# RWKV attention and top-1 experts on one core: when r and k are loaded, how row buffers are cleared and held, and the order of some VectorE steps

## The chip, the cores and the metric

The kernel runs on one core of a Trainium2 chip. A core has TensorE (matmuls, from SBUF into the banks of PSUM), VectorE, ScalarE and GpSimd (called PE, DVE, ACT and POOL in the profile), SyncE (SP), which here only issues transfers, and 16 DMA engines that move data between the chip's HBM and SBUF. The metric is the device time of one execution in microseconds (us), the median of several runs.

## What is computed

The reference is a linear attention with decay, followed by a layer of experts where each token goes to one expert. All data is float32.

```python
B, H, S, D = 4, 8, 768, 48           # batch, heads, sequence, head size
for t in range(S):                   # attention
    cur = einsum('bhd,bhe->bhde', u[None] * kt, vt)
    y[:, :, t] = einsum('bhd,bhde->bhe', rt, state + cur)
    state = w[None, :, :, None] * state + einsum('bhd,bhe->bhde', kt, vt)

x = y.transpose(0, 2, 1, 3).reshape(3072, 384)
logits = x @ w_gate                  # 8 experts
expert_idx = argmax(logits, axis=1)
gate_w = softmax(logits)[arange(3072), expert_idx]
for e in range(8):
    xe = x[expert_idx == e]
    out[expert_idx == e] = gate_w[...] * (maximum(xe @ w1[e], 0) @ w2[e])   # 384 -> 1024 -> 384
```

## The kernel before

The order of the work on every engine is the order in which the program is written: nothing is rescheduled. An engine runs its instructions one after the other, and each waits on semaphores for what it needs.

**Attention.** A turn `i` of the loop from L732 handles one unit: one batch `b` and one pair of heads `hp`, 16 units in all (U), four for each batch. Six chunks of 128 tokens are worked at once. In turn i:

- SP loads r and k of unit i + 3 (`load_rk`, L91) into one of three tiles `rks`, at the turn's beginning, and v and k of unit i + 3 (`load_vk`, L96) into one of four tiles `vks`, at its end. r and k come as 112 rows of 6 KB: 48 of the first head, 16 rows of zeros, 48 of the second. The arrays are laid out like that by the host. The three first loads are issued before the loop, load 3 at L720.
- TensorE makes the terms of a token with itself (`p_own`), the scores of each chunk (`p_scores`, L297), turns the outputs of unit i - 2 (`p_tr`, L358), makes the states (`p_ds`, L320), and the outputs of unit i - 1 (`p_out`, L340 and L345).
- VectorE scales r and k of unit i + 1 by the decays (`scale`, L266), lays the scores into masked matrices (`mask`), and scans the states. GpSimd forms r times k of unit i + 1 (`pairs`, L272) and scales its keys (`keys`, L276).
- ScalarE writes the diagonals (`diag`, L303), copies the outputs of unit i - 2 into a tile of rows (`keep`, L362), and copies the outputs of unit i - 1 from PSUM.

The tile of rows `xbs[b % 2]` collects the finished tokens of one batch from its four units. When a batch is full, VectorE picks each token's expert (`choose`, L368) and its place among that expert's tokens (`slots`), and GpSimd scatters the rows, 128 tokens at a time, to an array `rows` in HBM that has an area for each expert (`send`, L410; `sends` gives the turns: those of batch b in turns 4b + 6 to 4b + 9). The part of each area between rows 320 and 416 is cleared first (`clear`, L115, in turn 4), since a pass reads a fixed number of rows for each expert.

**Experts.** Two short passes `early` of 160 tokens for experts 0 and 1 fill the end of the attention. Eight passes `late` follow, k = 0 to 7, one for each expert and of a fixed width: `WIDTH` is 224, 192, 416, 412, 408, 396, 380, 364 (the loop from L905). While pass k does its first layer, the kernel has the second layer of pass k - 1 (called `o`) still to do.

From pass 2 on the first layer goes in four quarters (`quarter`, L493): a 2 x 2 product of blocks with seven instead of eight products, which takes sums of weight blocks `quart[q]` (`quarter_sums`, L533: five VectorE operations for a quarter) and sums of token blocks `toks` (`token_sums`, L545: four operations). The sums of pass k + 1 are made by VectorE during pass k: those of quarter q - 2 after quarter q, the rest after the last quarter, behind the transposes `xT` of pass k + 1's tokens (L470) and its token sums. Within a quarter VectorE does the steps L515, L519, L522, L523 and L525 on what TensorE has left in PSUM, and then the sums of pass k - 1's hidden values (`inner_sums`).

The second layer of the first 256 tokens of pass k - 1 is `tokens_out` (L586), again with seven products. It starts with four small VectorE operations, here called the places (L589 to L594): they compute to which row of the output each token goes, for the two scatters at its end. Then come the products (L603) in five banks ba, bb, bd, be, bf. Bank bf is the same as ba, so the last product waits until VectorE has read ba's second half, in the step `add` at L621. In `tokens_out` of pass 1, which runs after pass 2's quarters, ba and bf are the bank `dsb`.

Of the kernel before, what the change touches and what calls it, by code (L numbers as in the profile page):

```python
# [40 lines left out]
def bc(ap, shape):  # L41
    return ap.to_broadcast(shape)


def straight(tc, rk, vk, w, w1, w2, out, flag):
# [45 lines left out]
    def load_rk(i):  # L91
        if i < U:
            b, hp = divmod(i, HP)
            nc.sync.dma_start(rks[i % 3][0:KP], rk[b, hp].rearrange("h p u s -> (h p) u s")[0:KP])

    def load_vk(i):  # L96
        if i < U:
# [14 lines left out]
    nz = (CAP - PAD) * HP * Q // 128  # L112
    zt = ca.tile([128, nz], FP32, name="zt")

    def clear():  # L115

        nc.gpsimd.memset(zt, 0.0)
        nc.sync.dma_start(rows.rearrange("(e n) c -> e (n c)", e=E)[:, PAD * HP * Q:CAP * HP * Q].rearrange(
            "e (p z) -> p e z", p=128), bc(zt[:, None, :], [128, E, nz]))

    p_fill(17, X01[1][:, 0, :])
    strict = cp.tile([128, C], FP32, name="strict")
# [126 lines left out]
    Ss = [ca.tile([128, D, G - 1], FP32, name=f"S{i}") for i in range(2)]  # L249
    own = [ca.tile([128, G, 32], FP32, name=f"own{i}") for i in range(2)]  # L250
    yTs = [ca.tile([128, 2, S // 2], FP32, name=f"yT{i}") for i in range(3)]
    xbs = [ca.tile([128, G, HP, Q], FP32, name=f"xb{i}") for i in range(2)]
    lg, sub, ex, eq = [ca.tile([128, G, E], FP32, name=n) for n in ("lg", "sub", "ex", "eq")]
    rko = ca.tile([128, G, E], FP32, name="rko")
    mx, se, m2 = [ca.tile([128, G], FP32, name=n) for n in ("mx", "se", "m2")]
# [104 lines left out]

    def keep(i):
        b, hp = divmod(i, HP)  # L362
        nc.scalar.copy(xbs[b % 2][:, 0:4, hp, :], trv[0])
        nc.scalar.copy(xbs[b % 2][:, 4:G, hp, :], trv[1])

    full = [128, G, E]

    def choose(b):  # L368
        oh = ohs[b % 2]
        nc.vector.tensor_reduce(lg, xbs[b % 2][:, :, :, 2 * D:].rearrange("p c a e -> p c e a"), axis=AX, op=ALU.add)  # L370
        nc.vector.tensor_reduce(mx, lg, axis=AX, op=ALU.max)
        nc.vector.tensor_tensor(sub, lg, bc(mx[:, :, None], full), op=ALU.subtract)
        nc.scalar.activation(ex, sub, func=ACT.Exp)

        nc.vector.scalar_tensor_tensor(out=eq, in0=sub, scalar=0.0, in1=bc(rev[:, None, :], full),
                                       op0=ALU.is_equal, op1=ALU.mult)
        nc.vector.tensor_reduce(m2, eq, axis=AX, op=ALU.max)
        nc.vector.tensor_tensor(oh, eq, bc(m2[:, :, None], full), op=ALU.is_equal)
# [10 lines left out]
                             skip_group_check=True)  # L389

    def slots(b):
        oh, xb = ohs[b % 2], xbs[b % 2]
        nc.vector.tensor_tensor(rko, rp, oh, op=ALU.mult)
        with nc.allow_low_precision("whole numbers below 2^24"):
            nc.vector.tensor_reduce(slot[b % 2], rko, axis=AX, op=ALU.add)

    def gates(b):
        xb = xbs[b % 2]
# [11 lines left out]
    def send(b, cs):  # L410
        for c in cs:
            s_ = nc.gpsimd.indirect_dma_start(  # L412
                out=rows[:, :], out_offset=bass.IndirectOffsetOnAxis(ap=slot[b % 2][:, c:c + 1], axis=0),
                in_=xbs[b % 2][:, c].rearrange("p a q -> p (a q)"), in_offset=None, bounds_check=E * N - 1, oob_is_err=False)
            tc.declare_no_dep(s_.ins, group="rows", reason="each token has a row of its own")
            tc.add_to_no_dep_group("rows", s_.ins)

    def ids(b):
        nc.gpsimd.iota(xbs[b % 2][:, :, :, 2 * D + 1].bitcast(I32), pattern=[[4 * C, G], [1, HP]], base=4 * S * b,
                       channel_multiplier=4)  # L420

    def p_count():
# [18 lines left out]
    class Pass:  # L441
# [144 lines left out]
        def tokens_out(self):  # L586

            nt, it2 = self.nt, self.it2
            nc.vector.tensor_scalar(out=vt[:, 0:nt], in0=pos2[:, 0:nt], scalar1=float(self.s0),  # L589
                                    scalar2=bp[:, self.k:self.k + 1], op0=ALU.add, op1=ALU.is_lt)  # L590
            nc.vector.memset(it2[:, 0:nt], 1 << 20)
            nc.vector.tensor_scalar(out=ia[:, 0:nt], in0=self.xg[:, 0:nt, 1].bitcast(I32), scalar1=2, scalar2=None,  # L592
                                    op0=ALU.logical_shift_right)
            nc.vector.copy_predicated(it2[:, 0:nt], vt[:, 0:nt], ia[:, 0:nt])  # L594

            h, ws, g = self.h, w2s[self.k % 2], self.xg[:, :, 0:1]
            Z = DM // 2

            def product(p, at, a, b):
                for f in range(FT // 2):
                    nc.tensor.matmul(p[:, at * Z:(at + 1) * Z], lhsT=a(f), rhs=b(f), start=f == 0, stop=f == FT // 2 - 1,  # L603
                                     skip_group_check=True)
# [12 lines left out]

            y = self.yt

            def add(o, p, at, q):  # L620
                nc.vector.tensor_tensor(o, p[:, at * Z:(at + 1) * Z], q, op=ALU.add)  # L621
# [12 lines left out]
            ba, bb, bd, be, bf = self.banks  # L634
            product(ba, 0, A(0, 0), B_(0, 0))
            product(ba, 1, A(0, 1), B_(1, 0))
            nc.scalar.copy(so[0], ba[:, 0:Z])  # L637
            add(so[1], ba, 1, so[0])
            weigh(place(0, 0), so[1], 0)
            product(bb, 0, Sm(1), Tm(1))  # L640
            product(bb, 1, Sm(0), Tm(0))
            add(so[2], bb, 0, so[0])
            add(so[3], bb, 1, so[2])
            weigh(so[4], so[3], 0)
            weigh(so[5], so[3], 1)
            product(bd, 0, Sm(3), B_(1, 1))
            final(0, 1, bd, 0, so[4])
            scatter(out, it2[:, 0:1], self.yt[0][:, :], N)
            product(be, 0, Sm(2), Tm(2))
            add(so[6], be, 0, so[2])  # L650
            weigh(so[7], so[6], 1)
            final(1, 1, be, 0, so[5])
            product(bf, 0, A(1, 1), Tm(3))
            final(1, 0, bf, 0, so[7])
            scatter(out, it2[:, 1:2], self.yt[1][:, :], N)
# [148 lines left out]
    nc.gpsimd.tensor_copy(turn, xbs[1][0:1, G - 1, 2, 0:1])  # L804
    send(B - 2, range(3, G))
    p_out(U - 1)
    out_t(U - 1)
# [86 lines left out]

    for k, p in enumerate(late):
        o = late[k - 1]
        ahead = k + 1 < n and k > 0
        if k == n - 1:
            o.inner_sums()
# [10 lines left out]
        else:  # L910

            if k < 2:
                if k:
                    o.inner_sums()
                for f in range(FT):
                    p.L1((f,))
                    if f % 2:
                        result(p, f)
            else:
                for q in range(4):  # L920
                    p.quarter(q)
                    o.inner_sums((q,))
                    if q > 1:
                        late[k + 1].quarter_sums(q - 2)
                    if k == 2 and q % 2:
                        result(p, 2 * q - 1)
                p.relus()
            late[k + 1].xT()
            if ahead:
                late[k + 1].token_sums()  # L930
                for q in range(0 if k == 1 else 2, 4 if k < n - 2 else 3):
                    late[k + 1].quarter_sums(q)
            if k == 0:
                okay()
# [528 lines left out]
```

## Time and profile before

The median of six runs is 369.05 us. One more execution was profiled; the profile's numbers are of that one.

| what | value |
|---|---|
| median of 6 runs | 369.05 us (366.51 to 370.15) |
| the profiled execution's own time | 367.62 us |
| its span, first to last instruction | 365.7 us |
| mean granted TensorE clock | 0.995 |
| busy: TensorE, VectorE, ScalarE, GpSimd | 353.0, 261.5, 142.7, 203.8 us |
| HBM read, written | 53.29 MB, 11.40 MB |

The stages in the span: first loads and decays until about 16 us, the attention loop until about 110 us, its end with the early passes until about 142 us, passes 0 and 1 until 160 us, passes 2 to 7 until about 343 us, and the last second layer and scatter until the end.

In the views of the profile L12 is line 12 of the program. `a<-b` means that an instruction writes tile a and reads tile b. A waits view lists, for each engine and line, which engine's step ended the wait, the total in us, how often, and the longest. A line of the timeline gives start, length, engine, line, operation, tiles, shape and count, and in brackets how long the engine idled before it and what ended that. A line of a table of stretches gives the length, then busy time (and number of instructions) of PE, PEld (TensorE's loading of weights), DVE, ACT and POOL, then TensorE's granted clock, the DMA engines' share of busy time and GB/s.

### The profile page before, as it was taken

How to read it: one execution, taken by the hardware profiler on the slowest of the kernel's cores; microseconds unless marked ns; L12 is line 12 of the kernel's file. 1: busy time of each engine (PE TensorE's matmuls, PEld its weight loads, DVE VectorE, ACT ScalarE, POOL GpSimd, SP SyncE). 2: the span in 40 equal slices, each digit the busy share in tenths (PEclk: the TensorE clock that was granted, in tenths of full speed). 3: DMA queues.
4: the chain of work that ended last, by engine and by line, in shares of the span. 5: the costliest groups of instructions: out<-in, count | busy, mean ns of one | idle time of the engine just before them, and what ended most of it. 6: DMA issues, size and time to landing. Idle time of an engine off the chain costs nothing.

```text
span 365.7 us, 9077 instructions
## 1 busy us (share of the span) xinstructions
PE 353.0 (97%) x3355; PEld 334.8 (92%) x3355; DVE 261.5 (72%) x653; ACT 142.7 (39%) x411; POOL 203.8 (56%) x242
## 2 busy tenths in 40 slices
PE   7899999999999999999998999999999999999991
PEld 7688888888889999999998999999999999999891
DVE  6987798798872348674797995896688588685531
ACT  2587878787784301322313312322221231113210
POOL 5387889989865420652116407905922951999341
PEclk9999999999999999999999999999999999999997
DMA  7999997887656976888449327524742953313401
GB/s 202 265 243 233 271 273 244 258 249 231 218 147 205 319 295 124 209 250 229 133 159 213 92 73 213 162 89 152 189 146 91 203 152 125 108 51 100 133 20 50
DMA packets 35205, 65.08 MB, mean 178 GB/s; under 512 B 18617, under 2 KB 19657, under 8 KB 35152
## 3 DMA queue, kind: packets, MB, share of 16 engines
q1 hardware_dynamic: 29648, 49.86, 50.8%
q0 software_dynamic: 3776, 9.84, 7.6%
q10 hardware_dynamic: 1728, 4.72, 3.7%
q8 instruction: 28, 0.46, 0.5%
q14 instruction: 25, 0.20, 0.2%
HBM read 53.29 MB, written 11.40 MB: 177 GB/s over the span
## 4 chain that ended last, share of the span: by engine, by line
PE 90%; DMA 4%; DVE 2%; SPq 1%; POOL 1%; issue 0%; POOLq 0%; DVEq 0%
PE X L501 12%; PE X L563 10%; PE X L479 8%; PE tr L603 7%; PE yps L603 7%; PE X L297 6%; PE yps L340 6%; PE yps L501 5%; PE tr L358 5%; DMA vk<-in_vk_dram 4%; PE yps L345 3%; PE tr L501 3%; PE dsb L501 3%; PE dsb L603 3%; PE yps L563 2%; PE dsb L320 2%
## 5 line engine op out<-in xcount | busy, mean ns | idle before, releaser
L675 POOL DMA_INDIRECT out_dram<-yo,ix x28 | 28.4, 1015 | 67.9 <-DVE ia L592 63.7
L303 ACT ACTIVATE A<-ident,own 128x128 f32<-128x128 f32 x192 | 57.9, 390 | 7.4 <-DVE own L289 7.0
L412 POOL DMA_INDIRECT rows<-xb,slot x24 | 30.3, 1262 | 12.6 <-issue 4.8
L563 PE MATMUL X<-hT,w2s 128*128 128x160 f32 (+5 forms) x288 | 36.5, 287 | 0.0
L563 PEld LDWEIGHTS X<-hT,w2s 128*128 128x128 f32 x288 | 36.2, 191 | 0.2
L603 PE MATMUL yps<-tums,sums 128*128 128x192 f32 x184 | 32.4, 326 | 0.0
L603 PEld LDWEIGHTS yps<-tums,sums 128*128 128x128 f32 x184 | 30.3, 190 | 0.0
L675 POOL DMA_INDIRECT out_dram<-yt,it x16 | 16.8, 1048 | 22.1 <-DVE so L621 10.9
L266 DVE TENSOR_TENSOR RK<-rk,TT 112x1536 f32<-112x1536 f32 x16 | 27.7, 1729 | 2.0 <-DMA rk<-in_rk_dram 2.0
L297 PEld LDWEIGHTS X<-RK 48*128 48x128 f32 x384 | 23.1, 187 | 6.3 <-issue 4.3
L297 PE MATMUL X<-RK 48*128 48x128 f32 x384 | 27.1, 283 | 1.2 <-DVE RK L266 1.2
L272 POOL TENSOR_TENSOR rp<-rk 112x768 f32<-112x768 f32 x15 | 27.3, 1819 | 0.0
L309 DVE COPY_PREDICATED A<-strict,X 128x512 f32<-128x512 int32 x32 | 23.3, 742 | 4.3 <-ACT A L303 4.2
L501 PE MATMUL X<-xT,w1s 128*128 128x208 f32 (+5 forms) x120 | 26.0, 331 | 0.0
L689 POOL TENSOR_TENSOR tums<-w2s,tums 128x384 f32<-128x384 f32 x24 | 24.7, 1029 | 0.4
L340 PE MATMUL yps<-A,vk 128*48 128x128 f32 x384 | 24.0, 274 | 0.0
L501 PEld LDWEIGHTS X<-xT,w1s 128*128 128x128 f32 x120 | 20.9, 190 | 0.0
L340 PEld LDWEIGHTS yps<-A,vk 128*48 128x48 f32 x384 | 20.2, 123 | 0.5
L637 ACT COPY so<-tr 128x192 f32<-128x192 f32 x7 | 2.2, 318 | 44.4 <-PE tr L603 44.4
L689 DVE TENSOR_TENSOR sums<-hT 128x512 f32<-128x512 f32 x16 | 17.1, 1068 | 3.2 <-ACT hT L481 3.2
L603 PE MATMUL tr<-w2s,hT 128*128 128x192 f32 x112 | 19.4, 326 | 0.0
L530 ACT ACTIVATE hT<-hT 128x416 f32<-128x416 f32 (+5 forms) x23 | 12.4, 537 | 17.9 <-DVE hT L522 17.8
(214 smaller groups left out, 828.2 us busy)
## 6 DMA issues: line engine op xcount, KB each, us to landing
w1s<-in_w_dram SPq DMA_DIRECT2D x36, 384.0 KB, 3.3
rk<-in_rk_dram SPq DMA_DIRECT2D x16, 672.0 KB, 8.9
w2s<-in_w_dram SPq DMA_DIRECT2D x24, 384.0 KB, 3.6
vk<-in_vk_dram SPq DMA_DIRECT2D x16, 528.0 KB, 5.5
w2s<-in_w_dram ACTq DMA_DIRECT2D x8, 384.0 KB, 5.7
xs<-rows SPq DMA_DIRECT2D x16, 169.0 KB, 5.3
w1s<-in_w_dram ACTq DMA_DIRECT2D x4, 384.0 KB, 3.6
rows<-zt SPq DMA_DIRECT2D x1, 1248.0 KB, 7.7
```

Of the source, the lines that this page charges most:

```text
L266: nc.vector.tensor_tensor(RKs[i % 3][0:KP].rearrange("p u (c t) -> p u c t", t=C), x[0:KP].rearrange("p u (c t) -> p u c t", t=C), bc(TT[: ...
L272: (eng or nc.gpsimd).tensor_tensor(rps[i % 2][0:KP], x[0:KP, 0], x[0:KP, 1], op=ALU.mult)
L297: nc.tensor.matmul(o, lhsT=r[q, 1, c * C:(c + 1) * C], rhs=r[q, 0, c * C:(c + 1) * C], start=True, stop=True, skip_group_check=True)
L303: nc.scalar.activation(A[:, place(c, h), :], ident, func=ACT.Copy, scale=own[i % 2][:, c, h:h + 1])
L340: nc.tensor.matmul(o(c, h), lhsT=v[:, c, h * D:(h + 1) * D], rhs=A[:, place(c, h), :], start=c < 2, stop=c == 0, skip_group_check=True)
L412: s_ = nc.gpsimd.indirect_dma_start(out=rows[:, :], out_offset=bass.IndirectOffsetOnAxis(ap=slot[b % 2][:, c:c + 1], axis=0), in_=xbs[b % ...
L479: nc.tensor.matmul(p[:, 0:self.n], lhsT=w1s[self.k % 2][f // 2][:, m, f % 2 * 128:(f % 2 + 1) * 128], rhs=self.t[:, m, 0:self.n], start=m ...
L501: nc.tensor.matmul(p[:, at * n:(at + 1) * n], lhsT=a, rhs=b, start=j == 0, stop=j == len(ab) - 1, skip_group_check=True)
L563: nc.tensor.matmul(p[:, 0:n], lhsT=w2s[self.k % 2][f // 2][:, f % 2, m * 128:(m + 1) * 128], rhs=self.h[:, f, self.c:self.n], start=f == 0 ...
L603: nc.tensor.matmul(p[:, at * Z:(at + 1) * Z], lhsT=a(f), rhs=b(f), start=f == 0, stop=f == FT // 2 - 1, skip_group_check=True)
L675: s_ = nc.gpsimd.indirect_dma_start(out=to[:, :], out_offset=bass.IndirectOffsetOnAxis(ap=at, axis=0), in_=x, in_offset=None, bounds_check ...
L689: (eng or nc.vector).tensor_tensor(o, a, b, op=how)
```

## The change

Loads of r and k: the first three are as before. The others bring only the 96 rows that are not zeros, as two transfers of 48 rows, one to partitions 0 to 47 and one to 64 to 111; the 16 rows between keep the zeros of the first three loads. In the loop load 4 is issued at the beginning of turn 1, and load i + 4 in turn i, after GpSimd's product for unit i + 1.

Clearing: instead of one transfer for eight experts in turn 4 there are four for two experts each, at the ends of turns 2 to 5. Tile of rows: three in place of two, so that batch b has `xbs[b % 3]`.

Order of VectorE's steps: in pass 2 (`k == 2`) the sums of pass 3's quarter q - 1 are made after quarter q, in place of those of q - 2, so that one quarter's sums, not two, are left for after the last quarter. In `tokens_out` the places are computed after the three `add` steps on ba and bb instead of at the start, in every pass.

```diff
     def load_rk(i):
         if i < U:
             b, hp = divmod(i, HP)
-            nc.sync.dma_start(rks[i % 3][0:KP], rk[b, hp].rearrange("h p u s -> (h p) u s")[0:KP])
+            if i < 3:
+                nc.sync.dma_start(rks[i % 3][0:KP], rk[b, hp].rearrange("h p u s -> (h p) u s")[0:KP])
+            else:
+                for h in range(2):
+                    nc.sync.dma_start(rks[i % 3][64 * h:64 * h + D], rk[b, hp, h, 0:D])
...
-    def clear():
-        nc.gpsimd.memset(zt, 0.0)
-        nc.sync.dma_start(rows.rearrange("(e n) c -> e (n c)", e=E)[:, PAD * HP * Q:CAP * HP * Q].rearrange(
-            "e (p z) -> p e z", p=128), bc(zt[:, None, :], [128, E, nz]))
+    def clear(e):
+        if not e:
+            nc.gpsimd.memset(zt, 0.0)
+        nc.sync.dma_start(rows.rearrange("(e n) c -> e (n c)", e=E)[e:e + 2, PAD * HP * Q:CAP * HP * Q].rearrange(
+            "e (p z) -> p e z", p=128), bc(zt[:, None, :], [128, 2, nz]))
...
-    xbs = [ca.tile([128, G, HP, Q], FP32, name=f"xb{i}") for i in range(2)]
+    xbs = [ca.tile([128, G, HP, Q], FP32, name=f"xb{i}") for i in range(3)]
...
         def tokens_out(self):
             nt, it2 = self.nt, self.it2
-            nc.vector.tensor_scalar(out=vt[:, 0:nt], ...)
-            nc.vector.memset(it2[:, 0:nt], 1 << 20)
-            nc.vector.tensor_scalar(out=ia[:, 0:nt], ...)
-            nc.vector.copy_predicated(it2[:, 0:nt], vt[:, 0:nt], ia[:, 0:nt])
+            def places():
+                nc.vector.tensor_scalar(out=vt[:, 0:nt], ...)
+                nc.vector.memset(it2[:, 0:nt], 1 << 20)
+                nc.vector.tensor_scalar(out=ia[:, 0:nt], ...)
+                nc.vector.copy_predicated(it2[:, 0:nt], vt[:, 0:nt], ia[:, 0:nt])
...
             add(so[3], bb, 1, so[2])
             weigh(so[4], so[3], 0)
             weigh(so[5], so[3], 1)
+            places()
             product(bd, 0, Sm(3), B_(1, 1))
...
     for i in range(1, U):
         b, k = divmod(i - 6, 4)
         rt = i >= 6 and k == 0 and b < B - 1
-        load_rk(i + 3)
+        if i == 1:
+            load_rk(4)
         p_own(i)
...
             pairs(i + 1)
+            load_rk(i + 4)
             keys(i + 1, nc.vector if i in (7, 8, 11, 12) else None)
...
         load_vk(i + 3)
-        if i == 4:
-            clear()
+        if 2 <= i < 6:
+            clear(2 * i - 4)
...
     for k, p in enumerate(late):
         o = late[k - 1]
+        lag = 1 if k == 2 else 2
...
                 for q in range(4):
                     p.quarter(q)
                     o.inner_sums((q,))
-                    if q > 1:
-                        late[k + 1].quarter_sums(q - 2)
+                    if q >= lag:
+                        late[k + 1].quarter_sums(q - lag)
...
                 late[k + 1].token_sums()
-                for q in range(0 if k == 1 else 2, 4 if k < n - 2 else 3):
+                for q in range(0 if k == 1 else 4 - lag, 4 if k < n - 2 else 3):
                     late[k + 1].quarter_sums(q)
```

More of the change, by code (lines that the diff above doesn't have):

```diff
@@ L362, in keep @@
         b, hp = divmod(i, HP)
-        nc.scalar.copy(xbs[b % 2][:, 0:4, hp, :], trv[0])
-        nc.scalar.copy(xbs[b % 2][:, 4:G, hp, :], trv[1])
+        nc.scalar.copy(xbs[b % 3][:, 0:4, hp, :], trv[0])
+        nc.scalar.copy(xbs[b % 3][:, 4:G, hp, :], trv[1])
     full = [128, G, E]
@@ L369, in choose @@
         oh = ohs[b % 2]
-        nc.vector.tensor_reduce(lg, xbs[b % 2][:, :, :, 2 * D:].rearrange("p c a e -> p c e a"), axis=AX, op=ALU.add)
+        nc.vector.tensor_reduce(lg, xbs[b % 3][:, :, :, 2 * D:].rearrange("p c a e -> p c e a"), axis=AX, op=ALU.add)
         nc.vector.tensor_reduce(mx, lg, axis=AX, op=ALU.max)
@@ L391, in slots @@
     def slots(b):
-        oh, xb = ohs[b % 2], xbs[b % 2]
+        oh, xb = ohs[b % 2], xbs[b % 3]
         nc.vector.tensor_tensor(rko, rp, oh, op=ALU.mult)
@@ L397, in gates @@
     def gates(b):
-        xb = xbs[b % 2]
+        xb = xbs[b % 3]
         nc.vector.tensor_reduce(se, ex, axis=AX, op=ALU.add)
@@ L413, in send @@
                 out=rows[:, :], out_offset=bass.IndirectOffsetOnAxis(ap=slot[b % 2][:, c:c + 1], axis=0),
-                in_=xbs[b % 2][:, c].rearrange("p a q -> p (a q)"), in_offset=None, bounds_check=E * N - 1, oob_is_err=False)
+                in_=xbs[b % 3][:, c].rearrange("p a q -> p (a q)"), in_offset=None, bounds_check=E * N - 1, oob_is_err=False)
             tc.declare_no_dep(s_.ins, group="rows", reason="each token has a row of its own")
@@ L418, in ids @@
     def ids(b):
-        nc.gpsimd.iota(xbs[b % 2][:, :, :, 2 * D + 1].bitcast(I32), pattern=[[4 * C, G], [1, HP]], base=4 * S * b,
+        nc.gpsimd.iota(xbs[b % 3][:, :, :, 2 * D + 1].bitcast(I32), pattern=[[4 * C, G], [1, HP]], base=4 * S * b,
                        channel_multiplier=4)
@@ L588, in tokens_out @@
             nt, it2 = self.nt, self.it2
-            nc.vector.tensor_scalar(out=vt[:, 0:nt], in0=pos2[:, 0:nt], scalar1=float(self.s0),
-                                    scalar2=bp[:, self.k:self.k + 1], op0=ALU.add, op1=ALU.is_lt)
-            nc.vector.memset(it2[:, 0:nt], 1 << 20)
-            nc.vector.tensor_scalar(out=ia[:, 0:nt], in0=self.xg[:, 0:nt, 1].bitcast(I32), scalar1=2, scalar2=None,
-                                    op0=ALU.logical_shift_right)
-            nc.vector.copy_predicated(it2[:, 0:nt], vt[:, 0:nt], ia[:, 0:nt])
+            def places():
+                nc.vector.tensor_scalar(out=vt[:, 0:nt], in0=pos2[:, 0:nt], scalar1=float(self.s0),
+                                        scalar2=bp[:, self.k:self.k + 1], op0=ALU.add, op1=ALU.is_lt)
+                nc.vector.memset(it2[:, 0:nt], 1 << 20)
+                nc.vector.tensor_scalar(out=ia[:, 0:nt], in0=self.xg[:, 0:nt, 1].bitcast(I32), scalar1=2, scalar2=None,
+                                        op0=ALU.logical_shift_right)
+                nc.vector.copy_predicated(it2[:, 0:nt], vt[:, 0:nt], ia[:, 0:nt])
             h, ws, g = self.h, w2s[self.k % 2], self.xg[:, :, 0:1]
@@ L803, in straight @@
     keep(U - 2)
-    nc.gpsimd.tensor_copy(turn, xbs[1][0:1, G - 1, 2, 0:1])
+    nc.gpsimd.tensor_copy(turn, xbs[(B - 1) % 3][0:1, G - 1, 2, 0:1])
     send(B - 2, range(3, G))
```

## The prediction

> **What bounds the kernel now.** I read the page's slices first, then the waits of TensorE, then the chain of waits and VectorE's timeline around the one late wait, then the DMA share of the first stage.
>
> ```profile
> PE   7899999999999999999998999999999999999991
> PEclk9999999999999999999999999999999999999997
> DMA  7999997887656976888449327524742953313401
> ```
>
> A slice is 9.14 us. TensorE is busy at 9 tenths or more from the third slice to the last but one, at full clock; DMA is near full in slices 2 to 8, the attention loop.
>
> ```profile
> PE X L110 <- POOL ident masks.py:199: 1.4, 1, 1.4
> PE X L297 <- DVE RK L266: 1.2, 1, 1.2
> PE dsb L603 <- DVE so L621: 1.2, 1, 1.2
> PE dsb L285 <- POOL rp L272: 0.8, 1, 0.8
> PE dsb L285 <- DVE rp L272: 0.2, 1, 0.2
> ```
>
> All that TensorE waits for, in us. Four of the five lie before 16.2 us, in work that the change leaves alone. The third is at 193 us. So a transfer or another engine is worth time only where it makes TensorE wait, and after 16.2 us that happens once.
>
> ```profile
> 187.33 1.51 DVE xT L470 x3
> 188.84 0.27 DVE toks L689
> 189.13 0.94 DVE toks L689 x3
> 190.30 1.11 DVE quart L689 x5
> 191.44 0.90 DVE quart L689 x4
> 192.33 0.14 DVE vt L589
> 192.75 0.28 DVE so L621
> 193.16 1.54 PE dsb L603 x8
> ```
>
> The chain there (start, length, work; small steps not copied) is all VectorE: after pass 2's last quarter it transposes pass 3's tokens, forms their sums, two quarters' weight sums (10 `quart` operations, 189.98 to 192.25), the places (L589 to L594, 192.25 to 192.66), and only then reads bank `dsb` in L621, which frees it for TensorE's last product.
>
> ```profile
> 177.98 0.59 DVE L515 TENSOR_TENSOR midu<-X,mida 128x416 f32<-128x416 f32 x1 [0.23 <-PE X L501]
> 179.67 0.38 DVE L519 TENSOR_TENSOR midv<-X,midu 128x208 f32<-128x208 f32 x1 [1.10 <-PE X L501]
> ```
>
> In pass 2's third quarter VectorE idles 0.23 and 1.10 us (brackets), waiting for TensorE.
>
> ```profile
> 20.00:30.00 10.00, 9.88 (x168) 8.30 (x166) 8.58 (x12) 8.39 (x27) 8.40 (x7) 1.00 1.04 236
> 39.00:48.00 9.00, 9.00 (x164) 7.45 (x162) 7.00 (x14) 6.41 (x20) 6.84 (x16) 1.00 0.95 297
> rk<-in_rk_dram SPq DMA_DIRECT2D x16, 672.0 KB, 8.9
> vk<-in_vk_dram SPq DMA_DIRECT2D x16, 528.0 KB, 5.5
> rows<-zt SPq DMA_DIRECT2D x1, 1248.0 KB, 7.7
> ```
>
> The last two numbers of a stretch are the DMA share and GB/s. Full-width transfers get about 297/0.95 = 313 GB/s. A turn of the loop is 6.22 us on TensorE (turns 4, 5 and 6 start with L297 at 34.37, 40.59 and 46.81 in the chain).
>
> **The change, part by part.**
>
> *One quarter's sums sooner, places later (pass 2 and after).* Removed from between the last quarter and L621: five `quart` operations, 189.98 to 191.13 in the timeline, 1.13 us, and the four operations of the places, 0.41 us. L621 then starts at 192.66 - 1.13 - 0.41 = 191.12 and ends 0.35 later, at 191.47. TensorE followed it by 0.15 (193.01 to 193.16), so it may go at 191.62. It is ready after the eight matmuls of `tr` begun at 190.54, at 0.162 us each (1.30 per eight in the chain): 191.84. The stall goes entirely, with 0.22 us to spare: **-1.32 us** (193.16 - 191.84). Bounds: 0, if the wait only moves, to 1.32; I take 1.32, of which the sums alone give 1.13 and the places the last 0.19. The five operations now run in the second quarter, before L515 at 177.98. They delay it by 1.13 - 0.23 - 0.08 (the overlap of two operations' spans), so it ends at about 179.4, before TensorE has what L519 needs at 179.67: covered by VectorE's 1.33 us of idle time; each us beyond would push L515 of the fourth quarter, whose bank TensorE takes 0.39 us after it is read (183.65, 184.04). The places now stand before L628, which idles for 0.62 us waiting for ScalarE or TensorE in every pass: nothing.
> What is late next? After 193 TensorE is gapless to 358, so the saving should reach the end.
>
> *r, k in mid-turn and in halves.* 13 loads of 672 KB become 26 of 288 KB: 96 KB less each, 0.31 us of DMA at 313 GB/s. 13 more issues at 0.31 to 0.42 us on SP, which is no link of the chain after 4.2 us. The wait on SP moves: load i+4 is asked for in turn i once POOL's product L272 for i+1 is done, against after the turn's end before; in turn 2 that is 25.6 against 27.0. Queued behind this wait on SP are load i+3 of v, k and the clearing; where POOL scatters rows (L272 ends at 59.18, v, k left at 58.75) they leave about 1 us later. A v, k load asked for at 26.9 is first used by POOL at 38.3: 11.4 us, against landings of 7 to 8.5 in these turns. So there is cover of about 3 us for v, k, and more for r, k. Loads that TensorE never waited for give nothing in this execution. In the loop one thing more: turn 3 took 6.59 us, 0.37 over its neighbours, with weight loading idle for 0.30 at 30.3 that the profile gives to "issue", while the DMA share was 1.0. Whether DMA makes it no row shows: 0 to 0.37, half taken, **-0.19**.
>
> The Trainium skill speaks against the halves: "SBUF — State Buffer", section "Can I just issue two DMAs to hit both halves?", says that transfers to partitions 0 to 63 and 64 to 127 serialize, and its table that half the partitions reach 8 of 16 ports, at 196 GB/s against 328. By that a load would take 2 x 1.5 us against 2.1, an estimate from that page; the sum would stay as it is, since a turn has room for 0.9 us. No run here shows a load of long rows on half the partitions.
>
> *Clearing in four parts.* The same 1248 KB, after turns 2 to 5, three more issues of 0.66 us on SP. POOL's first scatter (54.59) waits for the last part, asked for at about 46 with 1.45 MB at most ahead and in it, 4.6 us at 313 GB/s: about 52. POOL has 0.28 us after that scatter (L272 ends 59.18, TensorE takes it at 59.46). Nothing, with 2 us of cover. POOL's fill of `zt` (0.35 us) is two turns sooner, beside the same idle time.
>
> *Three tiles.* ScalarE's copies L363 and L364 of batch 2 waited on the scatters of batch 0, those of batch 3 on batch 1's. In turn 10 L364 idles 1.09 us against 0.83 in turn 6, perhaps for that; TensorE went from L297 to L340 in 3.84 us in both turn 7 and turn 11. Nothing; covered by ScalarE's idle time.
>
> *Beyond the profiled execution.* It took 367.62 us (span 365.7 and 1.9 around it), 1.43 under the median 369.05. What the other runs have more is not shown. Landings come within 0.1 us of use at 17.1 and 22.0 (third and fourth r, k load), so waits on loads are a candidate: 0 to 1.43, half taken, **-0.72**.
>
> Sum for the profiled execution: 367.62 - 1.32 - 0.19 = 366.1. For the median: 369.05 - 1.32 - 0.19 - 0.72 = **366.8 us**.
>
> **The rivals.**
>
> *B, only the stall at 193 goes*: 369.05 - 1.32 = 367.7. For it: no wait on a load in the profile after 12.4 us. Against: DMA share 1.0 and two landings with no slack.
>
> *C, the sums don't free it*: the five operations push the fourth quarter's L515 past its 0.39 us, or POOL holds VectorE up (one L689 of 0.68 us took 2.98 at 199.5, beside POOL's work). The stall moves: 368.6 to 369.4. Against: POOL does nothing between 176.2 and 182.2.
>
> *D, slower: halves make DMA the bound of the loop.* Small partial loads are slow here: `xs`, 32 partitions, 169 KB in 5.3 us (32 KB/us) against `w1s`, 128 partitions, 384 KB in 3.3 (116 KB/us). Part of that is short runs, so I price half the full rate, 157 GB/s: r, k 590 kB 3.8 us, v, k 541 kB 1.7, and a clearing part or a turn's scatters (320 kB) 1.0: 6.5 against 6.22, and with what 62 to 68 us show (share 0.87 at 257 GB/s, so 295 at most) 6.9. Some 0.68 us in each of 11 turns, 7.5, less 3.4 of cover for v, k: +4.1, so 369.05 - 1.32 + 4.1 = 371.8. It decides once a v, k load takes over 11.4 us to land. Against: 26 smaller transfers keep all engines fed and carry 14% less.
>
> *E, all the unknown waits go*: 369.05 - 1.32 - 0.37 - 1.43 = 365.9.
>
> **How the numbers follow.** Forecast A, 366.8 (its own range 366.0 to 367.5): 0.48; B 0.16; C 0.08; D 0.20; E 0.08. What a measurement of this kernel tells from no change is about 0.5%, 1.85 us: below 367.2 is faster. Of A 0.40 lies there, with E 0.48 faster; the rest of A with B and C is 0.32 within; D is 0.20 slower. The range takes in E, less a little for the spread of runs, and the near end of D: 365.2 to 370.4.
>
> **What would show it.** TensorE's wait "dsb L603 <- DVE so L621" is gone, L621 comes before the places, and from the last quarter of pass 2 to pass 3 is 1.3 us shorter. Turn 3 takes 6.2 to 6.6. VectorE's idle time at L519 in pass 2's third quarter falls from 1.10 to about 0.3. Loads of r, k land in under 10 us. Wrong would be: waits "RK <- DMA rk" or "Kd <- DMA vk" in the loop, turns over 6.3 us, a wait of POOL's first scatter on the clearing, or L603 waiting for another VectorE step.

## The result and the profile after

| | before | changed |
|---|---|---|
| median | 367.41 us (365.9 to 370.32, 79 runs) | 365.47 us (364.8 to 368.94, 37 runs) |
| profiled execution, its span | 367.62, 365.7 us | 365.2, 363.3 us |
| mean granted TensorE clock of that execution | 0.995 | 0.996 |
| HBM read | 53.29 MB | 52.02 MB |

The ratio is 0.9946, 95% interval [0.9932, 0.9961]: by the ratio 1.98 us faster, between 1.4 and 2.5. The six runs shown at first had a median 1.64 us above that of all 79. A run at a mean clock of 0.985 to 0.987 takes some 3 us more than one at 0.992 to 0.997 (367.7 to 368.9 us against 364.8 to 366.7 for the changed kernel), so a median of six can shift with how many of them are such.

What TensorE waits for in the changed kernel (the waits view: total, times, longest, in us):

```profile
PE X L115 <- POOL ident masks.py:199: 1.4, 1, 1.4
PE X L303 <- DVE RK L272: 1.4, 1, 1.4
PE dsb L291 <- POOL rp L278: 0.4, 1, 0.4
PE dsb L291 <- DVE rp L278: 0.2, 1, 0.2
```

The wait of 1.2 us on `so` is gone; the others lie before 16 us. (Lines shift: L297 is now L303, L501 L507, L603 L611, L621 L629, L519 L525.) The chain of waits from the last quarter of pass 2 to pass 3, all TensorE:

```profile
185.54 3.90 PE yps L611 x24
189.44 1.30 PE tr L611 x8
190.74 1.30 PE dsb L611 x8
192.04 3.83 PE X L507 x22
```

The eight matmuls of `dsb`, which had waited until 193.16, follow those of `tr` at once. VectorE's timeline in the same pass:

```profile
178.41 0.37 DVE L525 TENSOR_TENSOR midv<-X,midu 128x208 f32<-128x208 f32 x1 [0.29 <-PE X L507]
...
189.85 0.35 DVE L629 TENSOR_TENSOR so<-dsb,so 128x192 f32<-128x192 f32 x1
190.12 0.74 DVE L629 TENSOR_TENSOR so<-yps,so 128x192 f32<-128x192 f32 x2
...
191.10 0.16 DVE L602 COPY_PREDICATED it<-vt,ia 128x2 int32<-128x2 int32 x1
```

The third quarter's idle time fell from 1.10 to 0.29 us, which is where the five sums went. L629 has read `dsb` at 190.20, 0.54 us before TensorE takes the bank, and the places come after it.

Where the 2.4 us of the span went, by the starts of stages in the two profiles: turn 2 began 0.88 us sooner (20.61 against 21.49), turn 3 took 6.22 instead of 6.59, the first step of pass 2 to that of pass 3 took 24.57 (167.47 to 192.04) instead of 25.97 (168.73 to 194.70), and 0.26 us was lost after 327 us. All other stages agree within about 0.1 us.

The loads in the changed kernel (issues: count, KB, median us to landing):

```profile
vk<-in_vk_dram SPq DMA_DIRECT2D x16, 528.0 KB, 7.7
rk<-in_rk_dram SPq DMA_DIRECT2D x26, 288.0 KB, 6.1
...
rows<-zt SPq DMA_DIRECT2D x4, 312.0 KB, 8.9
```

Halves of r and k land sooner than the whole did (8.9), v and k later (7.7 against 5.5). In this profile TensorE, VectorE's scaling and GpSimd's keys wait for none of them in the loop.

### The profile page after: what moved, and what is told of

It is laid out like the page before. It is cut to its first block, busy times and chain, and to the rows that moved or that the text cites. A ratio compares the mean times of both kernels' runs of the same rounds, so it can differ in the third digit from the quotient of the medians.

```text
span 363.3 us, 9106 instructions
## 1 busy us (share of the span) xinstructions
PE 351.7 (97%) x3355; PEld 333.9 (92%) x3355; DVE 263.7 (73%) x653; ACT 142.8 (39%) x411; POOL 203.9 (56%) x242
## 3 DMA queue, kind: packets, MB, share of 16 engines
HBM read 52.02 MB, written 11.40 MB: 175 GB/s over the span
## 4 chain that ended last, share of the span: by engine, by line
PE 93%; DVE 2%; DMA 2%; POOL 1%; issue 0%; POOLq 0%; SPq 0%; ACT 0%; DVEq 0%
PE X L507 12%; PE X L569 10%; PE yps L611 9%; PE X L485 8%; PE tr L611 8%; PE X L303 6%; PE yps L346 6%; PE yps L507 5%; PE tr L364 5%; PE dsb L611 4%; PE yps L351 3%; PE tr L507 3%; PE dsb L507 3%; PE yps L569 2%; PE dsb L326 2%; PE X L364 2%
## 5 line engine op out<-in xcount | busy, mean ns | idle before, releaser
L611 PE MATMUL yps<-tums,sums 128*128 128x192 f32 x184 | 32.4, 326 | 0.0
L611 PEld LDWEIGHTS yps<-tums,sums 128*128 128x128 f32 x184 | 30.3, 190 | 0.0
L303 PEld LDWEIGHTS X<-RK 48*128 48x128 f32 x384 | 23.1, 187 | 6.6 <-issue 4.3
L303 PE MATMUL X<-RK 48*128 48x128 f32 x384 | 27.1, 283 | 1.4 <-DVE RK L272 1.4
L507 PE MATMUL X<-xT,w1s 128*128 128x208 f32 (+5 forms) x120 | 26.0, 331 | 0.0
L507 PEld LDWEIGHTS X<-xT,w1s 128*128 128x128 f32 x120 | 20.9, 190 | 0.0
L640 ACT ACTIVATE so<-so,xg 128x192 f32<-128x192 f32 x24 | 10.0, 450 | 25.2 <-DVE so L629 25.2
L611 PE MATMUL tr<-w2s,hT 128*128 128x192 f32 x112 | 19.4, 326 | 0.0
```

Of the source, the lines that this page charges most:

```text
L303: nc.tensor.matmul(o, lhsT=r[q, 1, c * C:(c + 1) * C], rhs=r[q, 0, c * C:(c + 1) * C], start=True, stop=True, skip_group_check=True)
L507: nc.tensor.matmul(p[:, at * n:(at + 1) * n], lhsT=a, rhs=b, start=j == 0, stop=j == len(ab) - 1, skip_group_check=True)
```

## The experiments

The kernels ran in four groups (the first four of the table, the next four, the next three, the last), each on one chip together with the kernel before. The chips differ: before took 366.97 us on one and 370.78 to 372.78 on three others. So totals are compared on one chip, and stages within profiles.

| kernel | median us | before, same chip | ratio, 95% interval | pass 2 to pass 3, us |
|---|---|---|---|---|
| sums_and_places | 369.47 | 370.83 | 0.9971 [0.9951, 0.9991] | 24.57 |
| sums_only | 370.06 | 370.83 | 0.9982 [0.9960, 1.0004] | 24.85 |
| places_only | 370.09 | 370.83 | 0.9969 [0.9947, 0.9991] | 25.57 |
| sums_later | 371.15 | 370.83 | 1.0004 [0.9983, 1.0025] | 26.41 |
| after_again | 365.07 | 366.97 | 0.9953 [0.9924, 0.9983] | 24.58 |
| loop_part | 366.93 | 366.97 | 0.9994 [0.9970, 1.0018] | 25.97 |
| first_loads_split | 369.77 | 366.97 | 1.0063 [1.0040, 1.0085] | 24.57 |
| halves_twice | 389.23 | 366.97 | 1.0607 [1.0558, 1.0656] | 24.57 |
| after_whole_rows | 369.05 | 370.78 | 0.9939 [0.9908, 0.9970] | 24.58 |
| whole_twice | 392.96 | 370.78 | 1.0564 [1.0519, 1.0610] | 24.57 |
| start_sooner | 376.02 | 370.78 | 1.0133 [1.0104, 1.0163] | 24.57 |
| decays_sooner | 370.28 | 372.78 | 0.9936 [0.9910, 0.9961] | 24.57 |

### VectorE's order, in four pieces

`sums_and_places` is the kernel before with both changes of VectorE's order and nothing else; `sums_only` and `places_only` have one each; `sums_later` goes the other way, with three quarters' sums left for the end.

```diff
+        lag = 1 if k == 2 else 2          # sums_later: 3 if k == 2 else 2
...
-                    if q > 1:
-                        late[k + 1].quarter_sums(q - 2)
+                    if q >= lag:
+                        late[k + 1].quarter_sums(q - lag)
...
             weigh(so[5], so[3], 1)
+            places()
```

> The kernel before with only the VectorE part of the change (pass 3's sums one quarter sooner in pass 2, the places behind the add steps). Theory (the stall at 193 us is what the change is worth): TensorE's wait 'dsb L603 <- DVE so' is gone, the step from pass 2's last quarter to pass 3 is 1.3 us shorter, and the time is 1.3 us under the kernel before, ratio about 0.9964. Rival (the attention loop gives the larger share): under 0.7 us.

> The kernel before with pass 3's sums one quarter sooner in pass 2, the places where they were. Theory: VectorE reaches L621 1.13 us sooner, the stall of 1.32 us shrinks to about 0.2 us, and the time falls by 1.1 us. Rival (the five operations push the second half of pass 2 back): the stall stays near 1.3 us or comes again in the fourth quarter, and the time is that of the kernel before.

> The kernel before with the places behind the add steps, the sums as they were. Theory: L621 comes 0.41 us sooner, the stall falls from 1.32 to about 0.9 us, the time by 0.4 us, since the places are worth only 0.19 where the sums have gone but their whole 0.41 where they have not. Rival (other passes gain from it too, as GpSimd's scatters wait for VectorE): over 0.8 us.

> The kernel before with pass 3's sums one quarter later in pass 2 (three quarters' sums left for after the last quarter in place of two). Theory: each quarter's sums are 1.13 us on the path, so the stall grows from 1.3 to 2.45 us and the time by 1.1 us. Rival (the order matters only by chance, with VectorE hidden): no change.

From pass 2 to 3 these took 1.40, 1.12 and 0.40 us less than before's 25.97, and 0.44 more. The two changes together give in the kernel before exactly the changed kernel's 24.57. What is left of the wait, first in places_only, then in sums_later:

```profile
PE dsb L604 <- DVE so L622: 0.8, 1, 0.8
```

```profile
PE dsb L603 <- DVE so L621: 1.6, 1, 1.6
```

1.2 less 0.4 leaves 0.8: the wait follows VectorE's work ahead of L621 one for one. sums_later was a miss in size: the five operations put behind the last quarter cost 0.44 us, not the 1.13 they take. VectorE's timeline of sums_later, at the first step of the fourth quarter:

```profile
184.90 0.58 DVE L515 TENSOR_TENSOR midu<-dsb,mida 128x416 f32<-128x416 f32 x1
```

and of the kernel before:

```profile
183.07 0.58 DVE L515 TENSOR_TENSOR midu<-dsb,mida 128x416 f32<-128x416 f32 x1
```

Counted from the pass's start (171.68 and 168.73) that is 13.22 against 14.34 us: without the sums ahead of it the fourth quarter's work begins 1.12 us sooner, and its transposes (L470) 0.69 sooner (17.82 against 18.51). 1.13 less 0.69 is the 0.44. An operation moved within a queue that is already late gives back part of its price at the place it left. By their intervals, which all overlap, the totals hardly tell these four apart (the medians of sums_and_places and sums_later lie furthest apart, 369.47 and 371.15); the stages do.

### The changed kernel again, and the loop's part alone

`loop_part` has the halves in mid-turn, the clearing in four and the three tiles, with VectorE's order as before.

```diff
+                for h in range(2):
+                    nc.sync.dma_start(rks[i % 3][64 * h:64 * h + D], rk[b, hp, h, 0:D])
...
+            load_rk(i + 4)
...
+        if 2 <= i < 6:
+            clear(2 * i - 4)
...
+    xbs = [... for i in range(3)]
```

> The changed kernel once more, beside the three others of this call. If the two changes of place in VectorE's order are its whole worth (the theory): ratio to before 0.994 to 0.997, pass 2 to 3 (first step of the first quarter to the same of pass 3) 24.57 us against 25.97, no wait of TensorE on `so`. The 0.88 us by which the first turns began sooner in its first profile are then another execution's chance and need not come back. If the loop's transfers carry part of it (the rival): the start of turn 14 to the start of turn 1 is shorter than in the kernel before by more than turn 3's 0.37 us, and the ratio is under 0.994 on a chip where the loop has waits.

> The halves in mid-turn, the clearing in four and the three tiles, without the two changes of VectorE's order. Theory: nothing waits on these in the kernel before, so ratio 0.999 to 1.001, turns of 6.22 us, the wait of TensorE on `so` at 1.2 us and 25.97 us from pass 2 to 3 as before; turn 3 may be 0.37 us shorter. Rival 1, loads that come late in most executions (the 0.72 us that the prediction put beyond the profiled execution): ratio 0.998 or less, a narrower spread of the times. Rival 2, halves at half rate: turns over 6.3 us, ratio 1.005 or more.

The changed kernel came out at 0.9953, with 24.58 us from pass 2 to 3. The loop's part alone is 0.9994 [0.997, 1.0018], 0.2 us less with 1.1 less to 0.7 more possible; its turns take 6.22 us and its wait is untouched:

```profile
PE dsb L608 <- DVE so L626: 1.2, 1, 1.2
```

Two waits on loads do occur in this kernel's loop, one of VectorE's scaling and one of GpSimd's keys:

```profile
22.29 1.76 DVE L271 TENSOR_TENSOR RK<-rk,TT 112x1536 f32<-112x1536 f32 x1 [0.55 <-DMA rk<-in_rk_dram]
32.33 1.21 POOL L281 TENSOR_TENSOR Kd<-vk,T 128x480 f32<-128x480 f32 x1 [0.92 <-DMA vk<-in_vk_dram]
```

TensorE waits for neither: it has no wait between 25 and 130 us.

The theory holds as far as these runs resolve it: the gain that they show is the wait's. The sooner start of the changed kernel's profile can't be put down to the change. Turn 2 began at 20.61 and 20.91 us in the two profiles of the changed kernel, at 21.22 in loop_part, and at 21.49, 21.31, 20.70, 21.73 and 20.71 in before and the four kernels above, five kernels with the same instructions up to there and 1.0 us between them. Turn 3's excess of 0.37 us can't be put down to the change either: with the old loop it was 0.37, 0, 0, 0.10 and 0.11 in these five profiles, with the new one 0 in after, after_again and loop_part.

### What a half costs

`halves_twice` is the changed kernel with each half fetched once more into a tile that nothing reads; `after_whole_rows` is the changed kernel with whole rows (zeros included) at the new place, and `whole_twice` that with each whole load fetched twice.

```diff
                 for h in range(2):
                     nc.sync.dma_start(rks[i % 3][64 * h:64 * h + D], rk[b, hp, h, 0:D])
+                for h in range(2):
+                    nc.sync.dma_start(spare[64 * h:64 * h + D], rk[b, hp, h, 0:D])
```

> The changed kernel with each half of r and k after the third load fetched once more into a spare tile that nothing reads: 26 more transfers of 288 KB, 590 kB a turn. At the full rate of 313 GB/s a turn then asks for 5.5 us of DMA time, with clearing or scatters 6.5, against 6.22 us of TensorE. Theory (halves at or near full rate): DMA share of 1.0 from 21 to 60 us, loads up to some us later, the loop 0 to 4 us longer, ratio to before 0.995 to 1.006. Rival (halves at half the rate, 157 GB/s): 3.8 us more of DMA time a turn, 10.3 in all, so the loop's 13 turns grow by up to 4 us each less the cover: 30 us or more, ratio 1.08 or more.

> The changed kernel, with the loads of r and k whole again (112 rows with the zeros, one transfer of 672 KB) at their new place in mid-turn. Theory (no load is waited for in the loop, and halves save bytes but no DMA time): ratio to before 0.993 to 0.997, the same as the changed kernel's; no wait on a load from 21 us on; from 60 to 85 us the DMA share is 0.80 to 0.85 at about 248 GB/s, where the changed kernel has 0.88 at 230. Rival (the halves free the DMA engines): DMA share above the changed kernel's, loads land later, turns over 6.22 us, ratio 0.997 or more.

> As halves_twice, but with whole rows: every load of r and k after the third is one transfer of 672 KB, and is fetched once more, whole, into a spare tile that nothing reads. This asks for 2.55 MB more than halves_twice did. Theory (a pair of halves, 590 kB at the 233 GB/s worked out from halves_twice, takes 2.5 us of all DMA engines, whole rows, 688 kB at 313 GB/s, 2.2): 13 turns x 2 x 0.33 us = 8.6 us less than halves_twice, so 15.6 us over the changed kernel, ratio to before 1.03 to 1.045. Rival (the bytes alone count, at the 262 GB/s that halves_twice moved when full): 9.7 us more than halves_twice, ratio 1.08 or more.

halves_twice missed on both sides: 24.2 us over after_again (389.23 - 365.07), where the theory had 0 to 4 and the rival 30 or more. DMA is now the bound, as the stretch from 60 to 85 us shows (length, busy time and count of PE, PEld, DVE, ACT, POOL; granted clock, DMA share, GB/s), in halves_twice:

```profile
60.00:85.00 25.00, 17.22 (x226) 14.61 (x226) 12.80 (x16) 10.51 (x33) 13.28 (x15) 0.73 1.04 262
```

and in whole_twice:

```profile
60.00:85.00 25.00, 16.45 (x224) 13.78 (x220) 11.12 (x16) 10.79 (x33) 15.01 (x16) 0.80 1.02 297
```

TensorE is busy for 17 of 25 us. What it waits for in halves_twice:

```profile
PE dsb L294 <- POOL rp L281: 8.1, 3, 7.1
PE dsb L329 <- POOL Kd L285: 4.4, 3, 2.7
```

and VectorE, which makes unit 8's keys in GpSimd's place, in turn 7 of that kernel:

```profile
68.45 0.66 DVE L285 TENSOR_TENSOR Kd<-vk,T 128x480 f32<-128x480 f32 x1 [6.60 <-DMA vk<-in_vk_dram]
```

GpSimd's keys wait for the same loads in five turns, 15.4 us in all. It is the load of v and k, queued behind the halves, that comes late, the mechanism of the prediction's rival D; but it takes a doubling to get there. whole_twice, on another chip, costs 23.9 us over after_whole_rows (392.96 - 369.05), the same, though its second copies are 17% larger (688 kB against 590): a pair of halves of 590 kB holds the DMA engines as long as a whole load of 688 kB. That lies between the theory's 15.6 us (halves dearer) and the rival's 34 (bytes alone count), and on neither. When DMA is full, halves move 262 GB/s and whole rows 297. The same shows where it is not full. From 60 to 85 us before, after and in after_whole_rows:

```profile
60.00:85.00 25.00, 25.00 (x431) 21.60 (x431) 21.89 (x37) 19.90 (x65) 22.83 (x22) 1.00 0.82 248
```

```profile
60.00:85.00 25.00, 25.00 (x432) 21.20 (x430) 21.05 (x39) 19.92 (x64) 22.94 (x22) 1.00 0.89 228
```

```profile
60.00:85.00 25.00, 24.77 (x431) 21.03 (x427) 21.52 (x37) 19.67 (x64) 22.95 (x21) 1.00 0.80 247
```

With halves fewer bytes move (228 against 248 GB/s) in no less of the engines' time (0.89 against 0.82). after_whole_rows, at 0.9939 [0.9908, 0.9970], is as fast as the changed kernel, as the theory had it: leaving out the zero rows is worth nothing that these runs show.

### The first loads in halves

The changed kernel with each of the three first loads in three transfers.

```diff
-                nc.sync.dma_start(rks[i % 3][0:KP], rk[b, hp].rearrange("h p u s -> (h p) u s")[0:KP])
+                for p0, p1 in ((0, D), (64, KP), (D, 64)):
+                    nc.sync.dma_start(rks[i % 3][p0:p1], rk[b, hp].rearrange("h p u s -> (h p) u s")[p0:p1])
```

> The changed kernel with each of the three first r, k loads in three transfers: 48 rows, 48 rows, the 16 rows of zeros. VectorE waits for the first of them (1.16 to 1.67 us of idle time ahead of the first scaling), so here the price of halves lies on the path. If parts run beside each other at the rate of the whole (theory): the first scaling starts 0 to 0.9 us later than in the changed kernel (two more issues of 0.42 us, the last one 0.84 later), ratio to the changed kernel 1.000 to 1.002. If the parts serialize at half the rate (rival, the skill's rule): the two halves take 3 us against 2.1 for the whole and each later load of the start is late too, so the first scaling starts 1.5 us later or more and turn 2 another 1 us later, ratio to the changed kernel 1.004 or more.

VectorE's first two scalings:

```profile
7.47 1.76 DVE L273 TENSOR_TENSOR RK<-rk,TT 112x1536 f32<-112x1536 f32 x1 [1.73 <-DMA rk<-in_rk_dram]
...
13.12 1.76 DVE L273 TENSOR_TENSOR RK<-rk,TT 112x1536 f32<-112x1536 f32 x1 [1.09 <-DMA rk<-in_rk_dram]
```

The first starts 0.3 to 0.5 us later than in the changed kernel (6.93 and 7.20), less than its two more issues take (three in 1.34 us against one in 0.42), and no later than in the kernel before (7.48): no price of the parts is seen there. But the kernel is 4.7 us slower than after_again (369.77 - 365.07), which only the rival had, and not through the first scaling. Unit 1's scaling starts 1.4 to 1.7 us later (11.43 and 11.73), since SP issues its load 0.9 us later. TensorE waits 2.2 us for the first scaling, not 0.8 to 1.4, and in the profiled execution its clock falls (the third number from the end):

```profile
5.00:11.00 6.00, 3.50 (x37) 2.62 (x35) 4.21 (x6) 0.00 (x0) 1.95 (x11) 1.00 1.04 211
11.00:13.00 2.00, 2.00 (x26) 1.53 (x27) 0.77 (x2) 1.89 (x7) 0.00 (x0) 0.63 0.88 179
13.00:15.00 2.00, 2.00 (x24) 1.69 (x21) 1.88 (x2) 2.00 (x8) 0.06 (x1) 0.50 1.18 291
15.00:17.00 2.00, 2.00 (x11) 2.00 (x11) 2.00 (x4) 0.13 (x1) 2.00 (x3) 0.50 1.00 161
17.00:20.00 3.00, 3.00 (x37) 2.45 (x38) 1.41 (x3) 0.70 (x3) 1.05 (x1) 0.78 1.05 265
```

Turn 2 starts at 23.64 against 20.91 us; 1.67 us more go in turn 4, which takes 7.89, after GpSimd waited until 36.45 (2.19 us) for a load of v and k. The clock is not the main part: such a fall takes some 0.009 off a run's mean clock (an estimate from the five lines), and the profiled run's is 0.984; but seven of the twelve runs had 0.992 to 0.996, and their median is still 369.46 us, where the nine runs of after_again at 0.993 to 0.996 have 365.01. What those seven lost the time to, the later loads or something else, stays open.

### A shorter start

In the two profiles of the changed kernel what is left of TensorE's waits is at the start, so two tries went there. `start_sooner` has the small load `wug` issued by ScalarE's queue, so that SP begins with r and k, and makes the keys' decays (L163) and unit 0's keys sooner. `decays_sooner` has only the second.

```diff
-    nc.sync.dma_start(wug, w)
+    nc.scalar.dma_start(wug, w)           # start_sooner only
...
     decays(0, HP)
+    key_decay(0, HP)
+    p_key_decay(0, 1)
     scale(0)
     pairs(0, nc.vector)
-    key_decay(0, HP)
...
     p_own(0)
+    keys(0, nc.vector)
     own_t(0)
-    p_key_decay(0, 1)
```

> The changed kernel with a shorter start, where TensorE's remaining waits are: ScalarE's queue issues the first small load (wug), so that SP issues the first r, k load 0.44 us sooner; VectorE makes the keys' decays (L163, 0.68 us) while it waits for that load instead of after it, and unit 0's keys (0.66 us) ahead of the diagonal's transpose, where it idled. If VectorE's work up to unit 1's scaling sets the start (theory): that scaling starts 0.5 to 1.3 us sooner (11.43 and 11.73 us in the two profiles of the changed kernel) and turn 2 with it (20.61 and 20.91 us); ratio to before 0.990 to 0.995. If the landing of the second or third load sets it (rival): the first scaling is sooner but VectorE then waits for unit 1's or 2's load, turn 2 starts at 20.4 us or later, ratio as the changed kernel's, 0.995.

> The changed kernel with only the order of VectorE's work at the start changed (the small load wug is first on SP again): the keys' decays (L163, 0.68 us) are made while VectorE waits 1.16 to 1.50 us for the first r, k load, and unit 0's keys (0.66 us) ahead of the diagonal's transpose, ahead of which VectorE otherwise idles about 0.6 us. Theory (VectorE's work between the first scaling and unit 1's sets the start, and start_sooner was slow through wug's landing alone): unit 1's scaling starts 0.9 us sooner after the first one than the 4.5 us of the changed kernel (6.93 to 11.43), so 3.3 to 3.8 us after it; turn 2 starts 0.6 to 1.2 us sooner against the first scaling than the 13.7 us of the changed kernel (6.93 to 20.61); ratio to before 0.990 to 0.995, no clock below 1.00 in the first 21 us. Rival (loads set the start): VectorE waits for the load of unit 1 or 2, turn 2 13.4 us or more after the first scaling, ratio as the changed kernel's, 0.995.

start_sooner is 7 us slower than after_whole_rows on the same chip, which neither its theory nor its rival had. VectorE's first use of `wug`:

```profile
6.78 0.17 DVE L134 TENSOR_SCALAR pw<-wug 112x4 f32<-112x4 f32 x1 [4.21 <-DMA wug<-in_w_dram]
```

The 33 KB, issued at 0.83, are used 5.95 us later; ahead of the large loads they landed 1.8 us after their issue. Everything that stands on the decays is late, TensorE waits 3.6 and 2.0 us, its clock is 0.50 from 13 to 22 us, and turn 2 starts at 27.73 us, 6.7 later than in after_whole_rows (21.02). In decays_sooner VectorE's work does move forward, and stops at the next load:

```profile
5.73 0.69 DVE L163 TENSOR_TENSOR T3c<-TT,pw 112x512 f32<-112x512 f32 x1
7.08 1.76 DVE L272 TENSOR_TENSOR RK<-rk,TT 112x1536 f32<-112x1536 f32 x1 [0.66 <-DMA rk<-in_rk_dram]
...
11.66 1.76 DVE L272 TENSOR_TENSOR RK<-rk,TT 112x1536 f32<-112x1536 f32 x1 [0.94 <-DMA rk<-in_rk_dram]
```

Unit 1's scaling starts 4.58 us after the first, as in the changed kernel (4.50), now waiting 0.94 us for its load; turn 2 starts 13.74 us after it, as in the changed kernel (13.7). The rival holds: in this kernel the second load's landing sets the start. In the changed kernel VectorE did not wait there, so its work and that landing come out at nearly the same time, and moving VectorE's work alone gains nothing. Its ratio of 0.9936 [0.9910, 0.9961] can't be told from the changed kernel's. No version was found that beats it.

## Why the prediction was right, and where it wasn't

It said 366.8 us, faster; it is 365.47, faster by about the smallest step that it called measurable. The time lies in the range, near its lower end.

*The stall at 193 us, -1.32: right, in size and mechanism.* 1.40 us went, 1.12 for the sums (1.13 predicted). The 0.08 beyond the 1.32 is in the eight matmuls of `dsb`: from their start to pass 3's first step they took 1.38 us after the wait (193.16 to 194.54) and take 1.30 without it (190.58 to 191.88). The places alone are worth 0.40 (their four operations were put at 0.41), and 0.28 once the sums have gone, where 0.19 had been left for them. L621 was to start 22.39 us after the pass's start (191.12 - 168.73) and started 22.38 after it (189.85 - 167.47); the third quarter's idle time was to fall to 0.3 and fell to 0.29. That the saving reaches the end held: all later passes begin sooner by the same amount.

*Turn 3, -0.19: not shown to be the change's.* The excess was 0 to 0.37 us with the old loop, 0.12 on average over five profiles, and 0 in three with the new one; so the loop's share in it can be some 0.1 us.

*Beyond the profiled execution, -0.72 for waits on loads: this step failed.* It asked what the median of 369.05 had that the profiled execution had not, and put half of it down to late loads. There was nothing to divide: the 369.05 was itself high, by 1.64 us, as told with the result, and the median of 79 runs, 367.41, is 0.21 below the profiled execution's 367.62. The loop's part alone shows no gain either, 0.2 us with an interval that holds zero (and, at 1.1 less to 0.7 more, does not by itself exclude 0.72). The error of the baseline and the wrong term pointed the same way, and the forecast of the ratio (366.8/369.05 = 0.9939) came out near the 0.9946 measured partly by that luck. By the measured baseline and the stall alone it would be 367.41 - 1.40 = 366.0; the further 0.5 us is within the ratio's interval (1.4 to 2.5 us in all), and whether the loop has a share in it stays open. By medians on one chip, VectorE's order alone took 1.36 us off, loop_part 0.04, the changed kernel 1.90, and after_whole_rows and decays_sooner, which have both parts, 1.73 and 2.50. And loop_part ran only where before took 366.97 us. On the slower chips TensorE waited in the loop with the old loads (in sums_only 1.2 us for ScalarE's `yT` and 1.2 for VectorE's scans) and with the new ones (0.6 and 0.9 in after_whole_rows); what the loop's part alone does there was not run.

*Halves and mid-turn loads, nothing: right for TensorE, though a number in it was wrong.* TensorE waited for no load, and turns 2 to 5 stayed at 6.22 us. The waits that the prediction named as a sign of being wrong did come in loop_part (0.55 and 0.92 us, as shown), covered by other work. But "0.31 us of DMA less each" didn't come true: a pair of halves takes as long as the whole. And the full rate of 313 GB/s isn't reached in a loop that is bound by DMA, which moved 262 with halves. 590 kB at that rate is 2.25 us a turn, and 13 of them made the loop 24.2 us longer, 1.86 a turn: so by this estimate the changed loop has some 0.4 us of DMA time to spare in a turn, not 0.9. The Trainium skill's rule ("SBUF — State Buffer", "Can I just issue two DMAs to hit both halves?") would make a pair of halves 3.0 us against 2.1, an estimate from the 196 and 328 GB/s at 1 MiB in the table of the same page, section "Door 1: The DMA port swizzle". Here a pair takes the time of a whole load, so it moves 590/688 = 0.86 of the whole's rate, where the page's figures make 0.60: the direction agrees, the size doesn't, and the measured one decides.

*Clearing, nothing: right.* The last part, issued at 44.7 us, landed 7.3 later, at 52.0, as predicted; GpSimd's first scatter started at 53.39, so the cover was 1.4 us rather than 2. (It idled 0.69 us ahead of it, 0.62 before.) The three tiles were tried only with the rest of the loop's part.

*The rivals.* B (only the stall goes) is what the stages show; its 367.7 was 1.7 too high through the baseline. D's mechanism is real, a late v, k load that GpSimd and TensorE wait for, but its price for halves (157 GB/s) isn't. C and E did not happen.

## What to carry to other kernels

Where one engine is gapless, look for its few waits, list what the engine it waits for does just before, and move that work into that engine's earlier idle time: here such a gain could be worked out to a tenth of a microsecond and be checked in the stage, where totals could hardly tell it. Don't explain the difference between one profiled execution and a median of six by a mechanism, unless the profile shows one. Leaving out bytes is worth something only if it shortens what the DMA engines do and something waits for them; and a small transfer that others depend on belongs ahead of the large ones in time: issued beside them, on another engine's queue, it came late here.

## What the runs showed of the hardware that was not expected

In the profiles TensorE's granted clock fell to 0.50 some microseconds after an idle time of 2.2 us (first_loads_split) and of 3.6 and 2.0 us (start_sooner), and was back at 1.00 by 20 and 22 us; at the start of the other kernels, with no wait over 1.7 us, it stayed at 1.00. That the waits made it fall is not shown by a run of its own. In start_sooner turn 2 came 6.7 us later, more than the time by which TensorE's two waits are longer than those of after_whole_rows (5.6 us in all against 1.5 and 0.6, so 3.5 longer). A load of 33 KB took 1.8 us ahead of the 672 KB loads, and was used 5.95 us after its issue when another engine's queue issued it beside them: a queue of its own did not let it pass. And two transfers of 48 rows hold the DMA engines as long as one of 112: doubled, they cost 24.2 and 23.9 us.
